# Three more random draws in a planner that writes out the instruction order, and the orders drawn again

## The chip, the cores and the metric

The kernel runs on one core of one Trainium2 chip. The metric is the device time of one execution in microseconds; the median of three runs is given. The engines are TensorE (PE, matmuls, with its weight loads PEld), VectorE (DVE), ScalarE (ACT), GpSimd (POOL) and SyncE (SP, which issues DMAs).

## The reference

`x` is 2048 rows of 512, in bf16. It is normalised, and two branches are computed from the normalised rows `xn` and multiplied:

```python
x = A_x
xn = _layernorm(x, axis=-1)
s = _A_ref(xn, A_wq, A_wk, A_wv, A_wo)   # attention
g = _silu(_B_ref(xn, B_w1, B_w2))        # silu(silu(xn @ w1) @ w2)
return x + s * g

# _A_ref: 32 heads of 16, which share one key and one value head
q = (x @ wq).reshape(B, S, 32, 16).transpose(0, 2, 1, 3)
k = x @ wk                               # [B, S, 16]
v = x @ wv
p = softmax(einsum("bhqd,bkd->bhqk", q, k) * 16 ** -0.5)
o = einsum("bhqk,bkd->bhqd", p, v)       # then heads side by side, @ wo
```

`w1` is 512 x 1792 and `w2` is 1792 x 512. The attention has 32 x 2048 x 2048 scores and as many exps, and they are nearly all of the work.

## The kernel before

**The work in tiles.** A score tile is 128 keys by 512 queries of one head. There are 32 groups (four chunks of 512 queries, four octets of heads, and two halves of an octet, even and odd heads), and 64 tiles in a group (four heads, 16 blocks of keys): 2048 score tiles. The score matmul (`s_mm`, L922 in the profile) contracts over 32 rows of the array, so up to four of them, for the four heads of a group, run side by side on the four *row* strips. Each writes a PSUM bank of its own; there are seven such banks. An eighth gathers the sums of probabilities times values of a group.

**Two ways for the exp.** A tile goes one of two ways from its bank. On the A way ScalarE takes the exp (`pa_sb`, L1819), one to three tiles in an instruction where their banks lie evenly. On the D way VectorE turns the scores into 16-bit integers, which read as bf16 are a coarse power of two (`db_sb`, L1059). When four such tiles have come together as a batch, three more copies of the batch are made with a small integer added (`ds_sb`): on GpSimd as 64-bit additions (L1268), or near the end of the last group on VectorE (L1262). The four copies, summed with four weights, give a good exp. So an A tile has one matmul with the values, a D tile four.

**The matmuls with the values** (L1348) fill 32 columns of the array each, and four, for the four heads, run side by side on the four *column* strips: a round. The products with `wq`, `w1`, `w2` and `wo` are cut in the same way (L553), a round for each 128 of the contracted dimension: four rounds for a product with `wq`, `w1` or `wo`, 14 with `w2`. The last step of such a product can also be done as four *pieces* (L660), each of which takes the place of a missing fourth tile in a visit of the row strips.

**Products.** They are called jobs: `q` (queries, with `wq`), `h` (first layer, `w1`), `z` (second layer, `w2`) and `w` (output projection, `wo`). A job holds a PSUM bank from its start until it is evicted: `q` by VectorE, `h` and `z` by a tanh on ScalarE (`t_sb`, L716) and a product on VectorE (L718). The jobs stand in a list with a `pace`, a place in the stream of score tiles ahead of which they don't begin.

**Who sets the order.** There is no order in the source. A planner, run when the kernel is built, simulates the five engines with durations and latencies of its own and places one instruction after another; each engine's list of instructions is what the chip gets, with semaphore waits for what an instruction depends on. What lies around the change:

- `Planner.best` (from L234): of an engine's ready tasks it takes the one with the lowest priority number, and the earliest in the list among equals.
- `do_S` (from L1063): places one visit of the row strips. It chooses the free banks, how many tiles go the D way, and, where only three banks are free, whether a piece of a job goes along. `PIECE_MIN` says how many steps must lie ahead for that: 4 for `z`, 9 for the other kinds, which have four steps and so never give a piece.
- `can_start` (from L1440): a job begins only where not more than `START_Z` = 4 (for `z`) or `START_H` = 11 (for other kinds) exp results wait for their matmul.
- `act_step` (from L1781): ScalarE takes a ready task of another kind (such as a tanh) ahead of the next exp, if that task is ready no later than the exp.
- `SEEDS` and `redraw` (L410): the planner's thresholds are disturbed at random. After each visit of the row strips `redraw` draws a few choices anew (`pick`), such as the number of D tiles or the bank of a job; every eight visits (`STRETCH`) the next number of `SEEDS` starts a new random sequence. So the list of seeds fixes the whole order.

Of the kernel before, what the change touches and what calls it, by code (L numbers as in the profile page):

```python
# [19 lines left out]
T_ISSUE, T_SWDGE = 450.0, 1000.0  # L20
J_BASE, J_END, MIXJ = 0.1, 1.0, 2
SEEDS = (
# [6 lines left out]
)  # L29
STRETCH, SPREAD = 8, 0.4  # L30
PIECE_MIN = {"z": 4, "h": 9, "q": 9, "w": 9}
# [33 lines left out]
PR_ZER, FIRST_T, T_ACT, K0_DV, Q0_DV = -2, 4, (1,), (), ()  # L65
PR_OTR, PR_OB = -1, -1
CHAIN, AHEAD_T, START_T = '', 0.3, 11
R_WANT, R_SPLIT, R_FIRST, R_LATE, R_TOL, R_BANK = 0.03, 0.03, 0.1, 0.1, 0.05, 0.2
NEAR, AHEAD = 18, 0.6
SWITCH, SKEW, S4 = 105.0, 10.0, 3.5  # L70
INF = float("inf")
# [13 lines left out]
START_Z, START_H = 4, 11  # L85
# [35 lines left out]
class Planner:  # L121
# [110 lines left out]
            task.on_place(task.op)  # L232

    def best(self, eng, t):  # L234
        now, soon = None, None
        for k, task in enumerate(self.tasks[eng]):
            r = self.avail(task)
            if r is None:
                continue
            if r <= t + 25.0:  # L240
                p = task.prio() if callable(task.prio) else task.prio
                key = (p if isinstance(p, tuple) else (p,), k)
                if now is None or key < now[0]:
                    now = (key, task, r)
            elif soon is None or r < soon[2]:
                soon = (0, task, r)
        return now, soon

    def finalize(self, new_sem):
# [66 lines left out]
def bass_recurrent_scan__grouped_kv_mqa__dense_activation_silu__prompt_kernel(  # L316
# [30 lines left out]
    with ExitStack() as es:  # L347
# [53 lines left out]

        pl = Planner()
        rng = [Random(SEEDS[0])] if SEEDS else []

        def vary(x):
            return x * (1.0 + SPREAD * (rng[-1].random() - 0.5)) if rng else x

        pick = dict(want=None, split=False, first=None, late=0.0, tol=0.0, early=0.0, abank=None, jbank=None)

        def redraw():  # L410
            if not rng:
                return
            r = rng[-1]
            pick.update(want=r.choice((0, 1, 2)) if r.random() < R_WANT else None, split=r.random() < R_SPLIT,
                        first=r.choice(("pv", "job")) if r.random() < R_FIRST else None,
                        late=r.random() * 200.0 if r.random() < R_LATE else 0.0,
                        tol=r.random() * 250.0 if r.random() < R_TOL else 0.0,
                        early=r.random() * 400.0 if r.random() < R_TOL else 0.0,
                        abank=r.random() if r.random() < R_BANK else None, jbank=r.random() if r.random() < R_BANK else None)
        outs = []  # L420
        PH.clear()

# [640 lines left out]
        def do_S(t):  # L1063
# [26 lines left out]
                late = []  # L1090
            if n == 3 and pl.mode != "S" and not late:
                for jb in active:
                    if jb.piece is not None and jb.pos > 0 and (jb.got or jb.end - 1 - jb.pos >= PIECE_MIN[jb.kind]):
                        pj = jb
                if pj is not None:
                    gap = min((i for i in range(4) if i not in pj.got), key=lambda i: (sum(len(left[gg, i]) for gg in range(st["gA"], min(st["gA"] + 2, NG))), i))
                    avoid.add(gap)
# [342 lines left out]
        def can_start(jb, pro):  # L1440
            near = not pro and closing()
            chain = CHAIN and not pro and jb.kind in CHAIN and any(
                not a.fixed and a.left == 0 and a.kind in "hz" and (a.ev is None or a.ev.op is None or a.ev.op.end > pl.clk[PE]) for a in active)
            if jb.pace > progress() + (AHEAD if near else AHEAD_T if chain else 1e-9):
                return False
            if any(p.op is None for p in jb.preds):
                return False
            if jb.gate is not None and not jb.gate():
                return False
            if not pro and not near and a_pressure() > (START_T if chain else START_Z if jb.kind == "z" else START_H):  # L1450
                return False
            if not jb.fixed:
                lim = 2 if pro else 1
                if len([a for a in active if not a.fixed and (a.left or not TWO)]) >= lim or not pool_free:
                    return False
                if TWO and not pro and len([a for a in active if not a.fixed]) >= 2:
                    return False
            return True
# [166 lines left out]
        def a_pressure():  # L1625
            return sum(1 for b in pa_busy if b)
# [154 lines left out]
        def act_step():  # L1781
# [10 lines left out]
            if q:  # L1792
# [15 lines left out]
                if n:  # L1808
                    q = q[:n]
                    s = min(free, key=lambda k: max(pl.ready(AC, (), [("pA", k + d)]) for d in range(n)))  # L1810
                    rx = pl.ready(AC, [("ps", u.bank) for u in q], [("pA", s + d) for d in range(n)])
            if now is not None and (rx is None or now[2] <= max(t, rx) or False):
                pl.place_task(now[1])
                return True
            if rx is not None and rx <= t + 25:
# [106 lines left out]
```

## Time and profile before

| | before |
|---|---|
| median of three runs | 665.55 us (665.44 to 666.94) |
| the profiled execution | 665.78 us, of which the span of instructions 663.9 us |
| busy PE, ACT | 652.8 us, 651.3 us |
| busy DVE, POOL | 611.2 us, 569.8 us |
| granted TensorE clock | 1.0 |

Busy time is the time in which an engine executes at least one instruction. Matmuls are pipelined, and their ends are modelled, so PE's busy time alone does not say how fast it works. The chain of waits goes back from the last instruction, at each step to what released it or to the instruction before it on its engine. In a group of instructions the name left of the arrow is what is written, the names right of it are what is read.

### The profile page before, as it was taken

Reading aid. Unit: us, or ns where it says so; the run is one execution under the profiler, and the core shown is the slowest. Engines: PE = TensorE matmul, PEld = TensorE weight load, DVE = VectorE, ACT = ScalarE, POOL = GpSimd, SP = SyncE. Lnnn points to the kernel's source line nnn. Section 1 sums busy time; section 2 is a strip of 40 time slices with the busy share of each in tenths; the row PEclk is TensorE's granted clock in tenths of the full one; section 3 lists DMA queues with packets and bytes.
Section 4 is the critical chain, followed back from the end, with each engine's and each line's share of the span. In section 5 each row is a group of like instructions: output and inputs, shape, how many; then the busy total and the mean of one; then the engine's idle time right before and its main releaser. Section 6 shows DMA issues by size and latency. Waiting matters only on the chain.

```text
span 663.9 us, 21102 instructions
## 1 busy us (share of the span) xinstructions
PE 652.8 (98%) x8927; PEld 188.5 (28%) x8928; DVE 611.2 (92%) x1081; ACT 651.3 (98%) x780; POOL 569.8 (86%) x568
## 2 busy tenths in 40 slices
PE   8899999999999999999999999999999999999997
PEld 3332222222222222222222222222222222222232
DVE  8999999999999999998999999999989999999974
ACT  7999999999999999999999999999999999999996
POOL 3059899999998898898999899899999999889983
PEclk9999999999999999999999999999999999999999
DMA  9500000000000000000000000000000000100000
GB/s 297 172 9 1 2 2 2 2 2 1 2 2 18 18 18 18 2 2 2 2 1 3 18 18 18 17 2 2 2 2 2 1 2 18 34 18 1 2 2 34
DMA packets 11500, 12.85 MB, mean 19 GB/s; under 512 B 1808, under 2 KB 10768, under 8 KB 11408
## 3 DMA queue, kind: packets, MB, share of 16 engines
q1 hardware_dynamic: 10784, 10.65, 5.0%
q8 instruction: 72, 1.18, 0.8%
q0 software_dynamic: 192, 0.46, 0.2%
q10 hardware_dynamic: 432, 0.39, 0.2%
q14 instruction: 20, 0.16, 0.1%
HBM read 8.95 MB, written 2.10 MB: 17 GB/s over the span
## 4 chain that ended last, share of the span: by engine, by line
PE 94%; DVE 3%; DMA 1%; issue 0%; ACT 0%; ACTq 0%; DVEq 0%
PE ps L1348 42%; PE ps L922 31%; PE ps L553 20%; DMA kt_sb<-kt_sb 1%; DVE db_sb L1059 1%; DMA ds_sb<-in_A_x_dram 0%; DVE stats_sb L493 0%; DVE xn_sb L528 0%; PE ps L595 0%; DVE kt_sb L609 0%; PE ps L569 0%; DVE fin_sb L772 0%; DVE xnT_sb L580 0%; DVE u_sb L718 0%; PE ps L687 0%
## 5 line engine op out<-in xcount | busy, mean ns | idle before, releaser
L1819 ACT ACTIVATE pa_sb<-ps 128x1024 bf16<-128x1024 f32 (+1 forms) x681 | 614.5, 1015 | 3.5 <-PE ps L922 2.5
L1268 POOL INT64_ADD ds_sb<-db_sb x552 | 561.8, 1040 | 52.2 <-DVE otr_sb L1408 29.1
L1059 DVE TENSOR_SCALAR db_sb<-ps 128x512 uint16<-128x512 f32 x740 | 476.0, 683 | 34.8 <-PE ps L922 19.8
L1348 PE MATMUL ps<-ds_sb,v_sb 128*32 128x512 bf16 x2220 | 259.3, 383 | 0.0
L922 PE MATMUL ps<-qt_sb,kt_sb 32*128 32x512 bf16 x2048 | 250.0, 384 | 5.1 <-DMA kt_sb<-kt_sb 1.5
L1348 PE MATMUL ps<-pa_sb,v_sb 128*32 128x512 bf16 x1312 | 230.1, 383 | 0.6 <-DVE var_sb L522 0.6
L1348 PE MATMUL ps<-db_sb,v_sb 128*32 128x512 bf16 x740 | 162.3, 384 | 0.0
L922 PEld LDWEIGHTS ps<-qt_sb,kt_sb 32*128 32x128 bf16 x2048 | 62.4, 90 | 275.9 <-ACT pa_sb L1819 147.5
L1348 PEld LDWEIGHTS ps<-ds_sb,v_sb 128*32 128x32 bf16 x2220 | 62.8, 95 | 62.0 <-issue 46.7
L553 PE MATMUL ps<-xnT_sb,w_sb 128*32 128x512 bf16 x896 | 70.8, 383 | 0.0
L1348 PEld LDWEIGHTS ps<-pa_sb,v_sb 128*32 128x32 bf16 x1312 | 56.4, 95 | 39.6 <-issue 29.2
L553 PE MATMUL ps<-w_sb,u_sb 128*32 128x512 bf16 x784 | 61.6, 383 | 0.0
L1348 PEld LDWEIGHTS ps<-db_sb,v_sb 128*32 128x32 bf16 x740 | 39.6, 94 | 24.1 <-issue 19.5
L716 ACT ACTIVATE t_sb<-ps 128x512 bf16<-128x512 f32 x72 | 44.9, 624 | 0.1
L660 PE MATMUL ps<-w_sb,u_sb 32*128 32x512 bf16 x112 | 43.1, 385 | 0.0
L718 DVE SCALAR_TENSOR_TENSOR u_sb<-t_sb,ps 128x512 bf16<-128x512 bf16 x56 | 38.4, 685 | 0.7
L1425 POOL DMA_DIRECT2D kt_sb<-kt_sb x4 | 2.3, 566 | 26.8 <-DVE kt_sb L609 16.3
L553 PEld LDWEIGHTS ps<-xnT_sb,w_sb 128*32 128x32 bf16 x896 | 18.0, 95 | 22.9 <-issue 16.3
L1404 DVE STREAM_TRANSPOSE f_sb<-ps 128x512 f32<-128x512 f32 x31 | 21.9, 707 | 2.1 <-PE ps L1348 2.0
L553 PEld LDWEIGHTS ps<-w_sb,u_sb 128*32 128x32 bf16 x784 | 14.8, 95 | 20.8 <-issue 17.0
L553 PE MATMUL ps<-wo_sb,on_sb 128*32 128x512 bf16 x256 | 19.3, 382 | 0.0
L553 PE MATMUL ps<-xnT_sb,wq_sb 128*32 128x512 bf16 x240 | 18.9, 383 | 0.0
(84 smaller groups left out, 178.2 us busy)
## 6 DMA issues: line engine op xcount, KB each, us to landing
w_sb<-in_B_w_dram SPq DMA_DIRECT2D x2, 1792.0 KB, 14.4
xr_sb<-in_A_x_dram SPq DMA_DIRECT2D x16, 128.0 KB, 2.5
out_dram<-ob_sb SPq DMA_DIRECT2D x15, 128.0 KB, 1.7
ds_sb<-in_A_x_dram SPq DMA_DIRECT2D x3, 512.0 KB, 6.7
wq_sb<-in_A_wq_dram SPq DMA_DIRECT2D x1, 512.0 KB, 4.8
wo_sb<-in_A_wo_dram SPq DMA_DIRECT2D x1, 512.0 KB, 16.8
kt_sb<-kt_sb POOLq DMA_DIRECT2D x4, 112.0 KB, 4.1
ds_sb<-in_A_x_dram SPq DMA_DIRECT2D x2, 128.0 KB, 2.8
```

What stands on the lines that cost most here:

```text
L553: last = h.matmul(bank(b)[32 * j:32 * (j + 1), 0:n], lhsT=lhs(j), rhs=rhs, start=start, stop=stop, tile_position=(0, 32 * j), skip_group_c ...
L660: return (lambda pe: pe.matmul(bank(b), lhsT=lhs(k, rows, 0, P), rhs=rhs(k, rows), start=False, stop=last, tile_position=(32 * i, 0), skip ...
L716: t1 = Task(AC, 490.0, lambda a: a.activation(t_sb[:, k, :], src, ACT.Tanh, scale=scale), [held], [("t", k)], 0, [t0])
L718: t2 = Task(DV, T_P, lambda v: v.scalar_tensor_tensor(out=dst, in0=t_sb[:, k, :], scalar=1.0, in1=src, op0=ALU.add, op1=ALU.mult), [held, ...
L922: return pe.matmul(bank(b), lhsT=kt_sb[32 * i:32 * i + 32, g % 2, kt * P:(kt + 1) * P], rhs=qt_sb[32 * i:32 * i + 32, (g // 2) % NQR, :], ...
L1059: bt.P[i] = pl.add(Task(DV, T_P, lambda v: v.tensor_scalar(db_sb[:, bt.b, i * NQ:(i + 1) * NQ], bank(b), 128.0 * LOG2E, 128.0 * (SHIFT_BET ...
L1268: whole["po"].append(pl.add(Task(PO, T_P64, lambda g, cols=cols: g.int64_add(ds_sb[:, s, cols].bitcast(U64), db_sb[:, bt.b, cols].bitcast( ...
L1348: h = pe.matmul(bank(OB)[32 * i:32 * (i + 1), cols], lhsT=lhs, rhs=rhs, start=s0, stop=s1, tile_position=(0, 32 * i), skip_group_check=True)
L1404: t1 = pl.add(Task(DV, T_TR, lambda v: v.transpose(f_sb[:, k, :], bank(OB)), [("ps", OB)], [("F", k)], 1, [norm.get(("m", g - 2))]))
L1425: kt1[c] = pl.add(Task(PO, T_SWDGE, lambda e: e.dma_start(kt_sb[DH:P, 1, cols], kt_sb[0:P - DH, 0, cols]), [("kt0", k) for k in range(4 * ...
L1819: op = pl.place(AC, 0.8333 * NQ * n + T_AF, lambda a: a.activation(pa_sb[:, s * NQ:(s + n) * NQ].rearrange("p (b n) -> p b n", n=NQ), ps3[ ...
```

## The change

The planner gets more to draw, and the list of seeds is another, with 86 numbers for 84:

- in 15% of the redraws (`R_PIECE`), the bounds for pieces are drawn: `h` and `q` may then give pieces from 1 or 2 steps ahead, `w` from 2 or 4, `z` from 2 or 3 (or, with 9, less often than before);
- in 15% (`R_START`) the bounds for beginning a job are drawn, 2, 3 or 6 for `z` and 7, 9 or 14 for the others;
- from 40 us of the planner's own time on, in 3% of the choices among several ready tasks (`R_TASK`) a random one is taken in place of the first;
- from the same time on, in 3% of the cases (`R_EXP`) in which another ready task of ScalarE would go ahead of a ready exp, the exp goes first.

As every draw comes from the same sequences and the seeds are others, nearly the whole order is new. The arithmetic, the tiles, the buffers and the transfers are the same.

```diff
 SEEDS = (
-    9089, 3239, 7631, 4203, 5265, 9254, 578, 7567, 7348, 3979, 6108, 5815, 448, 7213, 3040, 7407,
...
-    7651, 8908, 5708, 5817,
+    1291, 9250, 3587, 5855, 4291, 5471, 9169, 1197, 2615, 5657, 4085, 3409, 4598, 3191, 211, 2683,
...
+    5443, 9741, 7044, 5277, 4, 5503,
 )
-R_WANT, R_SPLIT, R_FIRST, R_LATE, R_TOL, R_BANK = 0.03, 0.03, 0.1, 0.1, 0.05, 0.2
+R_WANT, R_SPLIT, R_FIRST, R_LATE, R_TOL, R_BANK, R_PIECE, R_START = 0.03, 0.03, 0.1, 0.1, 0.05, 0.2, 0.15, 0.15
+R_TASK, R_EXP, T_FLIP = 0.03, 0.03, 40000.0
...
     def best(self, eng, t):
-        now, soon = None, None
+        now, soon, open_ = None, None, []
...
-                if now is None or key < now[0]:
-                    now = (key, task, r)
+                open_.append((key, task, r))
             elif soon is None or r < soon[2]:
                 soon = (0, task, r)
+        if open_:
+            now = min(open_, key=lambda x: x[0])
+            if len(open_) > 1 and R_TASK and self.rng and t > T_FLIP and self.rng[-1].random() < R_TASK:
+                now = open_[int(self.rng[-1].random() * len(open_))]
         return now, soon
...
+                        piece={"z": r.choice((2, 3, 9)), "h": r.choice((1, 2, 9)), "q": r.choice((1, 2, 9)), "w": r.choice((2, 4, 9))}
+                        if r.random() < R_PIECE else PIECE_MIN,
+                        start=(r.choice((2, 3, 6)), r.choice((7, 9, 14))) if r.random() < R_START else None)
...
-                    if jb.piece is not None and jb.pos > 0 and (jb.got or jb.end - 1 - jb.pos >= PIECE_MIN[jb.kind]):
+                    if jb.piece is not None and jb.pos > 0 and (jb.got or jb.end - 1 - jb.pos >= pick["piece"][jb.kind]):
...
-            if not pro and not near and a_pressure() > (START_T if chain else START_Z if jb.kind == "z" else START_H):
+            if not pro and not near and a_pressure() > (START_T if chain else (pick["start"] or (START_Z, START_H))[jb.kind != "z"]):
...
-            if now is not None and (rx is None or now[2] <= max(t, rx) or False):
+            if now is not None and (rx is None or now[2] <= max(t, rx)) and not (
+                    rx is not None and rx <= t + 25 and R_EXP and t > T_FLIP and rng[-1].random() < R_EXP):
                 pl.place_task(now[1])
```

More of the change, by code (lines that the diff above doesn't have):

```diff
@@ L403, in bass_recurrent_scan__grouped_kv_mqa__dense_activation_silu__prompt_kernel @@
         rng = [Random(SEEDS[0])] if SEEDS else []
+        pl.rng = rng
         def vary(x):
             return x * (1.0 + SPREAD * (rng[-1].random() - 0.5)) if rng else x
-        pick = dict(want=None, split=False, first=None, late=0.0, tol=0.0, early=0.0, abank=None, jbank=None)
+        pick = dict(want=None, split=False, first=None, late=0.0, tol=0.0, early=0.0, abank=None, jbank=None, piece=PIECE_MIN, start=None)
         def redraw():
@@ L418, in redraw @@
                         early=r.random() * 400.0 if r.random() < R_TOL else 0.0,
-                        abank=r.random() if r.random() < R_BANK else None, jbank=r.random() if r.random() < R_BANK else None)
+                        abank=r.random() if r.random() < R_BANK else None, jbank=r.random() if r.random() < R_BANK else None,
+                        piece={"z": r.choice((2, 3, 9)), "h": r.choice((1, 2, 9)), "q": r.choice((1, 2, 9)), "w": r.choice((2, 4, 9))}
+                        if r.random() < R_PIECE else PIECE_MIN,
+                        start=(r.choice((2, 3, 6)), r.choice((7, 9, 14))) if r.random() < R_START else None)
         outs = []
```

8 rows, old and new, of the table SEEDS are left out of this document.

## The prediction, on record before the run

> **What bounds the kernel now.** I read the page first, then the chain of waits in a short stretch, then busy time by stage, then the groups by shape, then the waits.
>
> ```profile
> span 663.9 us, 21102 instructions
> ...
> PE 652.8 (98%) x8927; PEld 188.5 (28%) x8928; DVE 611.2 (92%) x1081; ACT 651.3 (98%) x780; POOL 569.8 (86%) x568
> ...
> PE 94%; DVE 3%; DMA 1%; issue 0%; ACT 0%; ACTq 0%; DVEq 0%
> ```
>
> TensorE (PE) and ScalarE (ACT) are both busy 98% of the span. The chain of waits decides between them: 94% of it is PE, nothing is ACT. How tightly PE's work is packed is seen in a few microseconds of that chain, in order of time (start, length, what):
>
> ```profile
> 302.03 0.76 PE ps L1348 x12
> 302.79 0.33 PE ps L922 x4
> 303.12 0.76 PE ps L1348 x12
> 303.88 0.04 issue
> 303.92 0.39 PE ps L922 x3
> 304.31 0.55 PE ps L1348 x8
> 304.86 0.32 PE ps L922 x3
> ```
>
> PE alternates between two forms. L922 is a *score visit*: three or four score tiles that run side by side on row strips of the array, 0.32 us whatever their number. L1348 (and L553) is a *column visit*: rounds of four matmuls that run side by side on column strips. Eight matmuls (two rounds) take 0.55, twelve take 0.76. Two longer visits, from the chain of the whole run, give the price:
>
> ```profile
> 52.16 0.98 PE ps L1348 x16
> ...
> 68.23 1.19 PE ps L1348 x20
> ```
>
> Two rounds more than 0.55 are 0.98: 0.215 us a round, and 0.55 - 2 x 0.215 = 0.12 us for each column visit beside its rounds. These prices hold wherever PE isn't kept waiting; the piece at 303.12 shows a wait, 0.04 of "issue" and a score visit of 0.39 for 0.32, 0.11 us in all.
>
> ```profile
> 0.00:18.00 18.00, 14.10 (x203) 6.84 (x207) 15.31 (x60) 13.72 (x24) 6.37 (x13) 1.00 0.92 302
> 18.00:40.00 22.00, 19.67 (x295) 8.20 (x290) 20.18 (x56) 20.98 (x27) 2.58 (x4) 1.00 0.35 111
> 40.00:640.00 600.00, 598.99 (x8130) 166.05 (x8127) 562.91 (x940) 598.34 (x705) 550.60 (x542) 1.00 0.03 7
> 640.00:664.00 24.00, 20.06 (x312) 7.41 (x309) 12.79 (x27) 18.29 (x27) 10.23 (x11) 1.00 0.07 24
> ```
>
> Busy time by stage (columns: stretch, length, then PE, weight loads, DVE, ACT, POOL, then the granted clock, 1.00 throughout): in the middle 600 us PE is idle for 1.0 us and ACT for 1.7. So the time is PE's own work plus few waits. An order that PE works through is worth what it changes in PE's count of visits and rounds, and in the waits between them.
>
> **The change, part by part.** The arithmetic and the tiles stay; the draws decide who does what and when. The counts come from comparing the instruction orders of the two built kernels; PE's first 17 visits of any kind are the same, up to a score visit of two tiles where three stood (behind the 17.49 quoted below).
>
> *PE's static work.* Score visits rise from 638 to 645 (two tiles: 2 to 9; three instructions: 388 to 362; four: 248 to 274), +7 x 0.32 = +2.24 us. Column visits rise from 636 to 640, +4 x 0.12 = +0.48. Rounds fall from 1637.5 to 1624.5, -13 x 0.215 = -2.80. Sum: -0.1 us. The 13 rounds have two sources. Forty product matmuls, 24 with w1, 8 with wq and 8 with w2, now ride as a fourth row strip on score visits: ten rounds less. That is the first draw at work, the smaller bound for such pieces. And four tiles of exp go from the VectorE path to ACT; such a tile is summed in four pieces there (itself and three shifted copies) and in one on ACT, so 12 matmuls less, three rounds. One of 16 visits of full-array matmuls goes, with the same 148 matmuls in them: 0.1. PE is left at -0.2 us.
>
> *The other engines.* The groups by shape (busy us, mean ns, then idle before):
>
> ```profile
> L1819 ACT ACTIVATE pa_sb<-ps 128x1024 bf16<-128x1024 f32 x593 | 562.5, 1051 | 2.1 <-PE ps L922 1.2
> ...
> L1819 ACT ACTIVATE pa_sb<-ps 128x512 bf16<-128x512 f32 x73 | 41.3, 630 | 0.9 <-PE ps L922 0.8
> L1819 ACT ACTIVATE pa_sb<-ps 128x1536 bf16<-128x1536 f32 x15 | 21.9, 1483 | 0.5 <-PE ps L922 0.5
> L1767 ACT ACTIVATE pa_sb<-ps 128x256 bf16<-128x256 f32 x4 | 1.5, 412 | 0.0
> ```
>
> ```profile
> L1059 DVE TENSOR_SCALAR db_sb<-ps 128x512 uint16<-128x512 f32 x740 | 476.0, 683 | 34.8 <-PE ps L922 19.8 <-PE ps L660 9.5 <-POOL ds_sb L1268 1.0
> ...
> L1262 DVE TENSOR_SCALAR ds_sb<-db_sb 128x2048 uint16<-128x2048 uint16 x3 | 1.9, 667 | 0.0
> ```
>
> ```profile
> L1268 POOL INT64_ADD ds_sb<-db_sb x552 | 561.8, 1040 | 52.2 <-DVE otr_sb L1408 29.1 <-DVE ob_sb L784 11.3 <-PE ps L1348 6.4
> ```
>
> ACT gets 607 exps of two tiles for 593, 53 of one for 73, 14 of three for 15, and 2 quarter-size ones fewer. By busy time over count that is 14 x 0.949 - 20 x 0.566 - 1.46 - 0.75 = -0.3 us. An upper bound leaves the saved instructions out and charges four tiles at 1051 - 630 = 421 ns: +1.7. The nearest rows are the same shapes, so I take -0.3; either way ACT follows PE, whose chain doesn't run through it. The Trainium skill, "ScalarE: Activation LUTs" (section "What ACT_TABLE_LOAD costs"), gives 0.833 ns an element and 186 ns an instruction, of which back-to-back ones overlap by 93; by it four tiles more in nine instructions fewer are an estimated +0.9 us of ACT time, between the two ends.
>
> DVE loses four evictions, 4 x 476.0/740 = -2.6 us, and gets four more shifted copies at the end, 7 for 3, 4 x 1.9/3 = +2.5: nothing. POOL loses 7 shifts, 7 x 1.02 = -7.1 us, and has 52.2 us of idle time before them already: nothing. SP's queue, POOL's four copies of kt_sb and all stores keep their order.
>
> *The waits.* Here lies the unknown.
>
> ```profile
> PEld ps L922 <- ACT pa_sb L1819: 147.5, 349, 0.7
> ...
> ACT pa_sb L1819 <- PE ps L922: 2.5, 5, 0.8
> ```
>
> The 147.5 us belong to weight loads, which stand ready while the matmuls before them still run (the middle stage above has 1.0 us of idle PE for all of them); and ACT waits for scores for 2.5 us in all. What PE really loses follows from its sum. Its steady work runs from the first score to the last output round:
>
> ```profile
> 10.14 0.39 PE L922 MATMUL ps<-qt_sb,kt_sb 32*128 32x512 bf16 x3
> ...
> 17.49 0.39 PE L922 MATMUL ps<-qt_sb,kt_sb 32*128 32x512 bf16 x3 [1.50 <-DMA kt_sb<-kt_sb]
> ...
> 29.09 0.36 PE L625 MATMUL ps<-wv_sb,xnT_sb 128*128 128x16 bf16 x8
> 29.38 0.62 PE L1348 MATMUL ps<-pa_sb,v_sb 128*32 128x512 bf16 x8
> ...
> 659.24 0.38 PE L1603 MATMUL ps<-xr_sb,ident 128*128 128x512 bf16 x1 [0.16 <-issue]
> ```
>
> From 10.14 to 659.24 are 649.1 us. The visits cost 638 x 0.32 + 636 x 0.12 + 1637.5 x 0.215 = 632.5, less about 2 for the first key and query products, which lie ahead of 10.14; some 14 groups of eight small full-array matmuls at 29.38 - 29.09 = 0.29 add 4. So about 14 us are waits, an estimate. Up to 18 us the orders agree and the waits stay (1.50 of them for the copy of the keys): the first row of the stages has 3.9 us of idle PE, of which I put 3 behind 10.14. The row of 18 to 40 us shows 2.3 idle. The rest, about 9, is no idle time of a stage but spread over the middle and the end, mostly as losses of 0.1 like the one at 303.88.
>
> Of these 11 us the redrawn order replaces every one by waits of its own. Bounds: all gone, -11; or new ones. For the likeliest case I keep the middle as it is, since a kind of wait that the same rules make recurs in any order they make, and halve the 2.3 of the start: in the stretch after 18 us the changed order puts the key products between smaller score visits and does 16 matmuls with w1 where 48 stood, so scores wait less behind them: -1.1.
>
> Sum on the profiled execution's own time, 665.78 (span 663.9 and 1.9 around it): 665.8 - 0.2 - 1.1 = 664.5. That execution lies 0.2 above the median of the three runs, 665.55, so against the median the forecast is **664.3**, -0.2%. About 0.3% (2 us) is what a measurement of this kernel can tell from no change.
>
> **The rivals.**
>
> *Fewer waits (faster).* If the added draws let the order avoid half of the 11 us, PE gains 5.5 less the 1.1 counted: 660 to 663, at the middle 661.5. For it: equal work in both orders leaves waits as the one thing that more freedom can improve. Against it: most are 0.1 us, near the size of the cost of a visit itself.
>
> *Products that hold a bank longer (slower).* A product with w1 or wq has four steps; eight of them now do their last step as four pieces on four score visits. Those visits come one score visit and one column visit apart, 0.32 + 0.55 to 0.98, so the product ends four times 0.87 to 1.30, or 3.5 to 5.2 us, later and its PSUM bank, one of seven, comes free so much later. A score visit that finds one bank too few waits for the next exp: 0.42 to 0.95 us by ACT's rows. Eight times that is 3.4 to 7.6 on top of the sum's 664.5: 668 to 672. It decides the sign from 0.4 us lost at each of the eight, 3.3 in all, which ends over 2 us above the time now. Against it: 28 steps with w2 are done so already, and the middle has 1.0 us idle.
>
> *ACT as the bound.* ACT idles 1.7 us in the middle. If its stream sets the pace, its upper bound counts and PE's gain doesn't: 665.8 + 1.7 = 667.5, less than 0.3% up. The Trainium skill, "TensorEngine Tiling (Array Packing)" (section "PSUM Bottleneck"), says that with the array tiled fourfold the copying out of PSUM may become the bottleneck; by that rule this is the case to expect. The trace disagrees so far: the chain gives ACT 0%.
>
> That the draws act on nothing is excluded: the row pieces with w1 and wq are new.
>
> **How the numbers follow.** The forecast 0.39, fewer waits 0.35, longer-held banks 0.21, ACT as the bound 0.05. Faster is the second: 0.35; slower is the third: 0.21; the forecast and ACT's case lie within 0.3%: 0.44. The range reaches from 660.5, inside the second case, to 669, inside the third; the forecast's own range is 663 to 667, from the bounds of the waits at the start and of ACT's stream.
>
> **What would show it.** Right: PE's busy time within 1 us of 652.8; score visits at 0.32 and column rounds at 0.215 as now; PE idle about 1 in the middle; less than 2.3 idle between 18 and 40 us. Fewer waits: column visits of three rounds at 0.76 throughout, with few "issue" pieces in the chain, and a span under 661. Longer-held banks: waits of L922 on ACT's exps next to row pieces with w1 and wq. ACT as the bound: its share of the chain no longer 0. The sum is wrong if visits of two tiles cost more than 0.32, or if the time moves by over 2 us with PE's idle time unchanged.

## The result, and the profile after

| | before | changed |
|---|---|---|
| median | 665.50 us (665.24 to 667.40, 22 executions) | 664.63 us (664.12 to 666.04, 22 executions) |
| the profiled execution | 665.78 us | 664.51 us |

The ratio is 0.9984, with a 95% interval of 0.9977 to 0.9990: 0.16% less, 0.87 us between the medians, and so within the 0.3% that the forecast took for no change. In some executions of every kernel the mean granted clock is only 0.992 to 0.998, and many of these are longer (the kernel before, beside the repetition further down: a median of 667.22 us in 12 such executions, 665.61 in the 11 others). The page of the changed kernel, its busy times and the shares of its chain of waits (in this kernel the lines lie 8 or 9 higher: L930 is the score visit, L1356 and L561 are the column visits, L1828 is the exp):

```profile
span 662.7 us, 21093 instructions
...
PE 651.9 (98%) x8914; PEld 188.2 (28%) x8915; DVE 613.1 (93%) x1081; ACT 651.2 (98%) x771; POOL 562.2 (85%) x561
...
PE 92%; DVE 4%; ACT 2%; DMA 1%; issue 0%; ACTq 0%; DVEq 0%
```

PE is 0.9 us less busy, ACT 0.1, POOL 7.6, and DVE is 1.9 us busier. ACT has appeared in the chain, with 2%. The stages, with the same columns as before:

```profile
0.00:18.00 18.00, 14.09 (x211) 6.90 (x215) 15.39 (x60) 14.01 (x24) 6.36 (x13) 1.00 0.93 303
18.00:40.00 22.00, 19.95 (x270) 7.83 (x266) 19.93 (x55) 20.97 (x24) 4.01 (x6) 1.00 0.35 111
40.00:640.00 600.00, 599.09 (x8161) 166.30 (x8165) 562.32 (x936) 599.24 (x703) 543.44 (x535) 1.00 0.02 7
640.00:664.00 24.00, 18.76 (x288) 7.14 (x281) 15.47 (x31) 16.95 (x23) 8.43 (x9) 0.99 0.08 25
```

Between 18 and 40 us PE is idle for 2.05 us, where it was 2.33. In the middle 600 us it is idle for 0.9 (1.0 before), and ACT for 0.8 (1.7 before): in the new order ACT has as little idle time there as PE. The first score visit, the first one behind the copy of the keys, and the last one, in the timeline of PE (start, length, what):

```profile
9.89 0.39 PE L930 MATMUL ps<-qt_sb,kt_sb 32*128 32x512 bf16 x3
...
17.21 0.39 PE L930 MATMUL ps<-qt_sb,kt_sb 32*128 32x512 bf16 x3 [1.22 <-DMA kt_sb<-kt_sb]
...
652.10 0.39 PE L930 MATMUL ps<-qt_sb,kt_sb 32*128 32x512 bf16 x3
```

and the last one of the kernel before:

```profile
653.17 0.39 PE L922 MATMUL ps<-qt_sb,kt_sb 32*128 32x512 bf16 x3
```

The last score visit starts 1.07 us earlier. The first already starts 0.25 us earlier (9.89 for 10.14; up to there the orders are the same, so this is a difference of two executions), and the rest lies on the way. To see where, I took every visit of PE from the first to the last score visit, from its start to the start of the next visit, and took off the price that such a visit has when nothing holds it: 0.320 to 0.325 us for a score visit, by its tiles, and 0.116 + 0.216 a round for a column visit. What is left are PE's waits.

| us | before | changed |
|---|---|---|
| priced visits, first to last score visit | 625.5 | 625.9 |
| full-array visits | 8.8 | 8.7 |
| waits up to 18 us | 1.05 | 1.29 |
| waits from 18 to 40 us | 1.64 | 1.52 |
| waits from 40 to 640 us | 5.99 | 4.81 |
| all waits | 8.7 | 7.6 |
| from the last score visit to the end | 10.70 | 10.61 |

So the priced work rose by 0.4 and the waits fell by 1.1; in the middle alone they fell by 1.2. With 0.25 from the start and 0.1 each from full-array visits and the tail, this is the 1.2 us between the two spans. In the profile of the repetition the waits of the middle are 5.0, so that they are fewer than before doesn't hang on one execution.

Which waits became fewer is in the semaphores of the same traces. In the middle 90 visits of the kernel before, and 73 of the changed one, are followed more than 15 ns late, and in all of them the late one is a score visit behind a column visit. Nine in ten of these score visits start 45 or 46 ns after the last semaphore that they wait for, so what released it is what they waited for (these sums lie a little above the row of the table, since other visits are a few ns early):

| late score visits in the middle, and their lateness | before | changed | repetition |
|---|---|---|---|
| all | 90, 6.1 us | 73, 4.9 us | 73, 5.0 us |
| released by VectorE's eviction of a score tile (`db_sb`) | 79, 5.5 us | 61, 4.2 us | 61, 4.3 us |
| released by an exp on ScalarE (`pa_sb`) | 2, 0.1 us | 1, 0.2 us | 1, 0.2 us |

One of them, from the chain of the changed kernel; the score visit is 0.15 us late behind three evictions:

```profile
300.81 1.90 DVE db_sb L1067 x3
302.71 0.05 issue
302.75 0.39 PE ps L930 x3
```

So what the changed order gains in the middle is that fewer score visits wait for VectorE to empty a bank.

### The profile page after: what moved, and what is told of

The parts are those of the page before. It is cut to its first block, busy times and chain, and to the rows that moved or that the text cites. A ratio compares the mean times of both kernels' runs of the same rounds, so it can differ in the third digit from the quotient of the medians.

```text
span 662.7 us, 21093 instructions
## 1 busy us (share of the span) xinstructions
PE 651.9 (98%) x8914; PEld 188.2 (28%) x8915; DVE 613.1 (93%) x1081; ACT 651.2 (98%) x771; POOL 562.2 (85%) x561
## 4 chain that ended last, share of the span: by engine, by line
PE 92%; DVE 4%; ACT 2%; DMA 1%; issue 0%; ACTq 0%; DVEq 0%
PE ps L1356 41%; PE ps L930 31%; PE ps L561 20%; ACT pa_sb L1828 1%; DMA kt_sb<-kt_sb 1%; DVE db_sb L1067 1%; DVE xn_sb L536 1%; DVE stats_sb L501 0%; DMA ds_sb<-in_A_x_dram 0%; PE ps L603 0%; DVE xnT_sb L588 0%; DVE kt_sb L617 0%; DVE fin_sb L780 0%; PE ps L695 0%; DVE v_sb L642 0%
## 5 line engine op out<-in xcount | busy, mean ns | idle before, releaser
L1828 ACT ACTIVATE pa_sb<-ps 128x1024 bf16<-128x1024 f32 (+2 forms) x674 | 615.4, 1029 | 2.6 <-PE ps L930 2.0
L1276 POOL INT64_ADD ds_sb<-db_sb x545 | 554.3, 1038 | 59.7 <-DVE otr_sb L1416 28.2
L1067 DVE TENSOR_SCALAR db_sb<-ps 128x512 uint16<-128x512 f32 x736 | 475.1, 682 | 36.5 <-PE ps L930 17.7
L1356 PE MATMUL ps<-ds_sb,v_sb 128*32 128x512 bf16 x2208 | 270.9, 384 | 0.0
L930 PE MATMUL ps<-qt_sb,kt_sb 32*128 32x512 bf16 x2048 | 252.7, 384 | 3.7 <-DMA kt_sb<-kt_sb 1.2
L1356 PE MATMUL ps<-pa_sb,v_sb 128*32 128x512 bf16 x1315 | 244.8, 383 | 0.6 <-DVE v_sb L642 0.6
L1356 PE MATMUL ps<-db_sb,v_sb 128*32 128x512 bf16 x736 | 165.5, 384 | 0.0
L930 PEld LDWEIGHTS ps<-qt_sb,kt_sb 32*128 32x128 bf16 x2048 | 63.1, 91 | 276.9 <-ACT pa_sb L1828 151.9
L1356 PEld LDWEIGHTS ps<-ds_sb,v_sb 128*32 128x32 bf16 x2208 | 63.9, 95 | 62.7 <-issue 48.5
L1356 PEld LDWEIGHTS ps<-pa_sb,v_sb 128*32 128x32 bf16 x1315 | 58.7, 95 | 43.1 <-issue 32.4
L561 PE MATMUL ps<-xnT_sb,w_sb 128*32 128x512 bf16 x872 | 67.9, 382 | 0.0
L561 PE MATMUL ps<-w_sb,u_sb 128*32 128x512 bf16 x776 | 61.2, 383 | 0.0
L668 PE MATMUL ps<-w_sb,u_sb 32*128 32x512 bf16 x120 | 46.1, 385 | 0.0
L1356 PEld LDWEIGHTS ps<-db_sb,v_sb 128*32 128x32 bf16 x736 | 39.8, 95 | 20.5 <-issue 16.5
L726 DVE SCALAR_TENSOR_TENSOR u_sb<-t_sb,ps 128x512 bf16<-128x512 bf16 x56 | 38.2, 681 | 0.8
L561 PEld LDWEIGHTS ps<-xnT_sb,w_sb 128*32 128x32 bf16 x872 | 17.9, 95 | 21.3 <-issue 14.3
L561 PEld LDWEIGHTS ps<-w_sb,u_sb 128*32 128x32 bf16 x776 | 15.1, 95 | 21.3 <-issue 17.7
L561 PE MATMUL ps<-wo_sb,on_sb 128*32 128x512 bf16 x256 | 19.6, 382 | 0.0
L561 PE MATMUL ps<-xnT_sb,wq_sb 128*32 128x512 bf16 x232 | 18.1, 382 | 0.0
```

Source lines behind the costliest of these rows:

```text
L561: last = h.matmul(bank(b)[32 * j:32 * (j + 1), 0:n], lhsT=lhs(j), rhs=rhs, start=start, stop=stop, tile_position=(0, 32 * j), skip_group_c ...
L668: return (lambda pe: pe.matmul(bank(b), lhsT=lhs(k, rows, 0, P), rhs=rhs(k, rows), start=False, stop=last, tile_position=(32 * i, 0), skip ...
L726: t2 = Task(DV, T_P, lambda v: v.scalar_tensor_tensor(out=dst, in0=t_sb[:, k, :], scalar=1.0, in1=src, op0=ALU.add, op1=ALU.mult), [held, ...
L930: return pe.matmul(bank(b), lhsT=kt_sb[32 * i:32 * i + 32, g % 2, kt * P:(kt + 1) * P], rhs=qt_sb[32 * i:32 * i + 32, (g // 2) % NQR, :], ...
L1067: bt.P[i] = pl.add(Task(DV, T_P, lambda v: v.tensor_scalar(db_sb[:, bt.b, i * NQ:(i + 1) * NQ], bank(b), 128.0 * LOG2E, 128.0 * (SHIFT_BET ...
L1276: whole["po"].append(pl.add(Task(PO, T_P64, lambda g, cols=cols: g.int64_add(ds_sb[:, s, cols].bitcast(U64), db_sb[:, bt.b, cols].bitcast( ...
```

## The experiments

Except the repetition and the two that exchange planner and seeds, each run keeps the changed kernel's planned order and adds instructions to it, leaves some out or makes some narrower; the planner doesn't see the edit. An added instruction stands behind a chosen one of its engine. Next to the ratio to the kernel before stands the difference to the changed kernel (664.71 us, nine executions of its repetition) between medians of executions with a mean clock of at least 0.999; these are two to eight for each run. The runs were made in four sessions, and the kernel before has a median of 665.50 to 665.70 in them, so differences of 0.2 us in this column mean nothing.

| run | edit | time, ratio to before (95% interval) | against the changed kernel |
|---|---|---|---|
| after_again | none | 664.76, 0.9983 (0.9973 to 0.9992) | |
| pe32 | PE +6.9 us | 671.17, 1.0062 (1.0047 to 1.0077) | +6.5 |
| act14 | ACT +7.3 | 670.22, 1.0047 (1.0031 to 1.0064) | +5.5 |
| dve11 | DVE +7.7 | 668.44, 1.0033 (1.0022 to 1.0044) | +3.6 |
| pool13 | POOL +7.9 | 665.81, 0.9991 (0.9982 to 1.0001) | +1.1 |
| nopiece | no pieces of `w1`, `wq` | 666.51, 1.0005 (0.9995 to 1.0014) | +1.7 |
| newplan_oldseeds | new planner, seeds before | 677.75, 1.0178 (1.0159 to 1.0198) | +13.0 |
| oldplan_newseeds | planner before, new seeds | 674.00, 1.0118 (1.0102 to 1.0135) | +9.3 |
| peminus | PE -6.9 | 663.84, 0.9962 (0.9946 to 0.9979) | -1.9 |
| actminus | ACT -7.0 | 665.46, 0.9991 (0.9979 to 1.0003) | 0.0 |
| bothminus | PE -6.9, ACT -7.0 | 661.93, 0.9928 (0.9912 to 0.9944) | -2.8 |
| allminus | these and DVE -7.6 | 662.01, 0.9954 (0.9937 to 0.9970) | -2.8 |

**The repetition** of the changed kernel, beside the three runs that undo or exchange a part of the change:

> The changed kernel once more, beside the three below on the same chip: 664.5 to 665.0 us, 0.1 to 0.2% under the kernel before.

Measured 0.9983 (0.9973 to 0.9992): the small gain stands.

### More work on one engine

**TensorE.** 32 rounds of zeros, each right behind a full round with the values:

```diff
+        full = [o for o, ok in PVS if ok]
+        for o in full[16::len(full) // 32][:32]:
+            spare(PE, o, lambda pe: col4(pe, OB, lambda j: zer_sb[:, 32 * j:32 * (j + 1)], zer_sb[:, :], False, False), [zw])
```

> The changed kernel's own order, with 32 extra column rounds on TensorE spread over the run: four matmuls of zeros each, added into the bank of a group between two rounds, so the output is unchanged. Theory (PE's visits and rounds set the time): +32 x 0.215 = +6.9 us over the changed kernel, 671.5 us. Rival (ACT's stream sets it, PE has some slack): under +2 us. Rival (the loss is taken up by waits that PE has anyway): +3 us or less.

Measured +6.5 us for 32 x 0.215 = 6.9: nearly the whole. The price of a round stands, and nearly all of the added PE work is on the path.

**ScalarE.** 14 exps of 512 columns between those of the middle, into a tile that nobody reads:

```diff
+        exps = [o for o in pl.order[AC] if o.end - o.t0 > 850.0 and o.t0 > 30000.0]
+        for o in exps[20::len(exps) // 14][:14]:
+            prev = spare(AC, o, lambda a: a.activation(dump_sb[:, :], zer_sb[:, :], ACT.Exp), [zw] + ([prev] if prev else []))
```

> The changed kernel's own order, with 14 extra exps on ScalarE, each of 512 zeros in SBUF to a spare tile, about 0.5 us from start to start, 6.7 us of ACT time in all. Theory (PE sets the time, ACT follows it and has slack): each lengthens the wait of a score visit for a free bank, but ACT catches up; at most +2 us. Rival (ACT as the bound, or PE and ACT coupled so closely that neither has slack): +5 to +7 us.

Measured +5.5 us. In the trace each added exp takes 0.52 us to the start of the next instruction, 14 x 0.52 = 7.3 us in all, a little more than was expected. The theory that ACT only follows PE fell. The chain of waits, the added group, and two stages of this run (the profiled execution took 673.69 us, with a granted clock of 0.77 in its second stage, so its chain is read as to its kind, not its length):

```profile
ACT 68%; PE 27%; DVE 3%; DMA 1%; issue 0%; ACTq 0%
...
L1898 ACT ACTIVATE dump_sb<-zer_sb 128x512 bf16<-128x512 bf16 x14 | 9.0, 640 | 0.0
...
18.00:40.00 22.00, 20.47 (x227) 7.51 (x217) 16.93 (x49) 17.98 (x20) 1.05 (x2) 0.77 0.32 104
40.00:640.00 600.00, 594.85 (x8086) 165.07 (x8087) 557.97 (x929) 599.54 (x709) 537.64 (x529) 1.00 0.03 7
```

Between 40 and 640 us PE is idle for 5.2 us (0.9 without the edit) and ACT for 0.5. A chain that gave ACT 2% gives it 68% for 1% more work: the two engines had run at nearly the same pace all along. Read as above, the score visits that ACT's exps release late go from 0.2 us in the middle to 5.3; those that wait for VectorE's evictions stay near 4.2.

**VectorE** got 11 transposes of 701 ns, **GpSimd** 13 additions of 610 ns (half the usual size):

```diff
+            prev = spare(DV, o, lambda v: v.transpose(dump_sb[:, :], zer_sb[:, :]), [zw] + ([prev] if prev else []))
...
+            prev = spare(PO, o, lambda g: g.int64_add(
+                dump_sb[:, :].bitcast(U64), w2_sb[:, 0:2, :].rearrange("p a n -> p (a n)").bitcast(U64), 1), [w2w] + ([prev] if prev else []))
```

> The changed kernel's own order, with 11 extra transposes of a 128x512 tile of zeros on VectorE, 0.63 us from start to start, 6.9 us in all. Theory: VectorE is idle for 49 us and evicts one score tile in three; a transpose holds a bank back by 0.63 us once: +1 us or less. Rival (any engine's delay is passed on, since only seven banks lie between): +4 to +7 us.

> The changed kernel's own order, with 13 extra 64-bit additions on GpSimd of half the size of a shifted copy, about 0.52 us each, 6.8 us in all. Theory: GpSimd is idle for 100 us and its copies are summed long after they are made: 0 us. Rival (delay passed on): +3 us or more.

VectorE's added work, by its group in the profile,

```profile
L1898 DVE STREAM_TRANSPOSE dump_sb<-zer_sb 128x512 bf16<-128x512 bf16 x11 | 7.7, 701 | 0.0
```

cost 3.6 us, nearly half, and not the 1 at most that its 49 us of idle time suggested, but less than the rival's 4 to 7. GpSimd's cost 1.1 of 7.9, again between theory and rival. So VectorE's gaps don't take up the half of what is added: the late score visits that its evictions of score tiles release go from 4.2 us in the middle to 6.6.

### One part of the change undone

**The pieces.** The eight steps with `w1` and `wq` that ride on score visits as four pieces go back to a column round behind the last of these visits:

```diff
+        for (jb, k), ps4 in PIECES.items():
+            if jb.kind not in "hq":
+                continue
...
+            for o, held_, _ in ps4:
+                held_[0] = None
+            o = ps4[-1][0]
+            new = spare(PE, o, jb.whole(k, ps4[-1][2]), list(o.deps))
...
```

> The changed kernel's own order, in which the eight product steps with w1 and wq that ride as four row pieces on score visits are put back: the pieces are left out, and each step is one column round right behind the score visit that carried its last piece. Theory (rounds of PE cost what they take): +8 x 0.215 = +1.7 us, by what 32 extra rounds cost per round +1.6. Rival (a product that is finished in pieces holds its bank longer, and that costs more than the round): the product still ends at the same visit here, so the hold is the same and the rival too expects +1.7; a result at or under the changed kernel would say that a piece isn't free on a score visit.

Measured +1.7 us: the eight rounds, 8 x 0.215 = 1.7, and nothing else. The edit keeps the end of these products where it was, so it doesn't test how long they hold their banks; it shows that the pieces give their rounds back in full. What the hold costs is in the trace of the changed kernel. The four pieces of one product with `w1`, in the timeline of PE:

```profile
201.03 0.38 PE L668 MATMUL ps<-xnT_sb,w_sb 32*128 32x512 bf16 x1
...
201.91 0.39 PE L668 MATMUL ps<-xnT_sb,w_sb 32*128 32x512 bf16 x1
...
202.78 0.38 PE L668 MATMUL ps<-xnT_sb,w_sb 32*128 32x512 bf16 x1
...
203.65 0.38 PE L668 MATMUL ps<-xnT_sb,w_sb 32*128 32x512 bf16 x1
```

From the first to the last piece are 2.6 us, and 2.6 to 2.8 in all eight products. In these stretches, each with the five visits behind it, PE's visits are late by 0.4 us together, where the rival *longer-held banks* of the prediction charged 3.4 to 7.6.

**Planner and seeds exchanged.** The first has the changed planner with the seeds of before, the second the planner of before with the changed seeds (the first's edit is shown, from the changed kernel):

```diff
-    1291, 9250, 3587, 5855, 4291, 5471, 9169, 1197, 2615, 5657, 4085, 3409, 4598, 3191, 211, 2683,
...
+    9089, 3239, 7631, 4203, 5265, 9254, 578, 7567, 7348, 3979, 6108, 5815, 448, 7213, 3040, 7407,
...
```

> The changed planner with the seeds of before, so an order that nobody chose. Its counts against the changed kernel's: 637 score visits for 645, 633 column visits for 640, 1649.5 rounds for 1624.5, by the prices -8 x 0.32 - 7 x 0.12 + 25 x 0.215 = +2.0 us. Theory of the prediction (waits of the same kind recur in any order that these rules make): 666.6 us. Rival (the choice of the seeds is what keeps the waits small; the added draws do little): far more than the sum of the visits, 669 us or over.

> The planner of before with the seeds of the changed kernel, the mirror of the run above. Its counts against the changed kernel's: 638 score visits for 645, 635 column visits for 640, 1649.5 rounds for 1624.5, by the prices -7 x 0.32 - 5 x 0.12 + 25 x 0.215 = +2.5 us. Theory of the prediction (waits recur alike): 667.1 us. Rival (the choice of the seeds): 669 us or over. If only one of the two mirrors is bad, the draws matter, not the choice.

Measured +13.0 and +9.3 us: neither the draws nor the seeds are good by themselves. Of the first, the chain, ACT's waits for scores (us, times, longest) and the middle stage:

```profile
PE 67%; ACT 23%; DVE 5%; POOL 2%; DMA 1%; issue 1%; POOLq 0%; ACTq 0%; DVEq 0%
...
ACT pa_sb L1828 <- PE ps L930: 5.3, 14, 0.8
...
40.00:640.00 600.00, 595.92 (x8045) 166.18 (x8045) 553.92 (x925) 593.34 (x689) 537.37 (x529) 1.00 0.03 7
```

and of the second:

```profile
ACT pa_sb L1819 <- PE ps L922: 6.4, 18, 0.9
...
40.00:640.00 600.00, 597.31 (x8102) 166.63 (x8099) 562.23 (x939) 591.75 (x697) 545.04 (x537) 1.00 0.03 7
```

In both, PE and ACT are idle by turns: 4.1 and 6.7 us of the middle in the first, 2.7 and 8.3 in the second. By the same account of visits as above, the first has 16.6 us of waits, 627.2 of priced visits and 13.6 behind the last score visit; the second 12.7, 628.6 and 11.8. Set beside the 7.6, 625.9 and 10.6 of the changed kernel, nine of the 13 us and five of the nine are waits. Seeds that belong to another planner give an order that nobody chose. In these two the waits are not small, so the rules alone don't make them small; how the two lists in use were chosen, and how other lists would do, isn't on record.

### Less work on one engine

These leave work out, and tell whether the engine that the chain names is the one to relieve.

```diff
+        full = [o for o, ok in PVS if ok and L[o.idx - 1].mode == "C" and L[o.idx - 1].idx > 0]
+        for o in full[16::len(full) // 32][:32]:
...
+            L.remove(o)
...
+            w = NQ // 2 if len(ntanh) > 6 and len(ntanh) % 2 else NQ
+            t1 = Task(AC, 490.0, lambda a: a.activation(t_sb[:, k, 0:w], src[:, 0:w], ACT.Tanh, scale=scale),
```

The lines up to `L.remove` are the run without 32 rounds, the last two the one with half of 33 tanh; the third run has both.

> The changed kernel's own order without 32 of the rounds with the values, each from the middle of a group and of a column visit (the sums lack those tiles). Visits stay 645 and 640, rounds fall from 1624.5 to 1592.5: -32 x 0.215 = -6.9 us of PE. Theory A (PE alone sets the time; the price of an added round, 0.9 of its length, holds both ways): -6 us, 658.5. Theory B (PE and ACT are coupled through seven banks and ACT has almost no slack, as 14 added exps showed): ACT then sets the pace, -1 to -3 us.

> The changed kernel's own order, with 33 of the 72 tanh taken over half their columns only (the other half of the gate keeps an older value): 33 x 0.21 = -7.0 us of ACT. Theory A (PE alone sets the time): 0 to -0.5 us. Theory B (coupled): -1 to -4 us.

> Both edits of the two runs above in one kernel: 32 rounds with the values left out and 33 tanh over half their columns. Theory A (PE alone): the same as without the rounds alone, about -6 us. Theory B (coupled): more than the two alone together, up to -6.9 us.

Measured -1.9, 0.0 and -2.8 us: theory B holds for the first and the third, while ACT's relief alone gives nothing, as theory A said. Of the run with less PE work, the chain, its one piece between 299.08 and 304.58 us in order of time, and the middle stage:

```profile
ACT 46%; PE 45%; DVE 6%; POOL 1%; DMA 1%; issue 1%; DVEq 0%
...
299.08 5.50 ACT pa_sb L1830 x6
...
40.00:640.00 600.00, 597.38 (x8069) 164.78 (x8065) 561.72 (x937) 599.71 (x705) 546.10 (x537) 1.00 0.03 7
```

In the kernel before, the chain at 302 us was score and column visits by turns; here, in a stretch of the same time, it is six exps one behind the other. PE has 2.6 us of idle time in the middle, ACT is full to 0.3 us, and of the 6.9 us that PE gave 1.9 came through. With ACT relieved too, ACT has 2.2 us of idle time again and 4% of the chain:

```profile
PE 84%; DVE 9%; ACT 4%; POOL 1%; issue 1%; DVEq 0%
...
40.00:640.00 600.00, 597.61 (x8085) 165.33 (x8085) 561.83 (x940) 597.82 (x706) 546.97 (x537) 1.00 0.03 7
```

The gain is more than the two alone, but still under half of the dose. The account of visits says where the rest is: the priced visits fell from 625.9 to 619.0 as meant, and the waits rose from 7.6 to 11.2 (12.5 with PE alone). In the middle the late score visits that VectorE's evictions of score tiles release rose from 4.2 us to 7.1 (7.4 with PE alone), those that ACT's exps release from 0.2 to 0.7 (1.2). So most of what was lost is a wait for VectorE. The last run takes other work from VectorE; 28 of the 56 products that end a first-layer tile go over half the columns:

```diff
+            nu.append(kind == "h")
+            d = NQ // 2 if kind == "h" and sum(nu) > NFT and sum(nu) % 3 else NQ
...
-                out=dst, in0=t_sb[:, k, :], scalar=1.0, in1=src, op0=ALU.add, op1=ALU.mult),
+                out=dst[:, 0:d], in0=t_sb[:, k, 0:d], scalar=1.0, in1=src[:, 0:d], op0=ALU.add, op1=ALU.mult),
```

> The changed kernel with the 32 rounds left out and 33 tanh halved as in the run before, and besides 28 of the 56 products that end a first-layer tile (VectorE) over half the columns, at 418 ns (the row of 256 columns) for 681: 28 x 0.263 = -7.4 us of VectorE, so that the output misses those parts. All three engines that read or write the seven banks are then about 7 us lighter. Theory (TensorE, ScalarE and VectorE form one loop through the banks, and each takes over where another is relieved): the time falls clearly below the run without VectorE's part (ratio 0.9928, -3 us against the changed kernel), to -5 to -7 us against the changed kernel, ratio 0.988 to 0.991. Rival (what came back of the 7 us lies in the waits of a fixed order between TensorE and ScalarE; VectorE has its own slack): as without VectorE's part, ratio 0.992 to 0.994.

```profile
L731 DVE SCALAR_TENSOR_TENSOR u_sb<-t_sb,ps 128x512 bf16<-128x512 bf16 x28 | 19.0, 678 | 0.5 <-ACT t_sb L729 0.2
L731 DVE SCALAR_TENSOR_TENSOR u_sb<-t_sb,ps 128x256 bf16<-128x256 bf16 x28 | 11.6, 413 | 0.1
```

The group went from 38.2 us to 30.6, and the time stayed where it was: 661.93 us for 661.91, both medians taken as in the last column of the table. The ratio of 0.9954 lies above both expected ranges; between medians of executions with a mean clock of at least 0.999 it is 0.9944, and 0.9946 without VectorE's part. So the rival held as to the time: relieving these products gains nothing. VectorE's evictions of score tiles, which were not shortened, still release 7.0 us of late score visits. Whether shorter evictions, or a new plan for the lighter work, would give that time back was not tried.

## Why the prediction was right, and where its steps were not

**The size.** The forecast of 664.3 stood 1.2 us below the median of the three runs before, and 0.9 us was measured (664.63). Of its two terms, -1.1 for waits is what the account of visits gives. The other, -0.2 for PE's static work, came out as +0.4 (625.5 to 625.9), less 0.1 for full-array visits. The prediction's counts with its rounded prices gave -0.1 for visits; the account, with 0.116 and 0.216 and a price by the tiles of a visit, over the part between first and last score visit, gives +0.4. Half a microsecond of 626 is what such a table can resolve, and the 0.25 of the start, a difference of two executions, made up for much of it. That is luck, and so is the place from which the other term came.

**The place of the waits: wrong.** The prediction kept the middle as it is and halved the 2.3 us of idle PE between 18 and 40 us. That idle time fell by 0.3 and the waits in the stretch by 0.1; the middle gave 1.2. PE's stalls in the stretch, from the timeline of the kernel before (the bracket holds the idle time and what ended it),

```profile
20.96 0.39 PE L922 MATMUL ps<-qt_sb,kt_sb 32*128 32x512 bf16 x3 [0.29 <-ACT pa_sb L1819]
...
22.43 0.39 PE L922 MATMUL ps<-qt_sb,kt_sb 32*128 32x512 bf16 x3 [0.24 <-ACT pa_sb L1819]
...
28.77 0.39 PE L922 MATMUL ps<-qt_sb,kt_sb 32*128 32x512 bf16 x3 [0.40 <-DVE kt_sb L609]
...
30.52 0.39 PE L922 MATMUL ps<-qt_sb,kt_sb 32*128 32x512 bf16 x3 [0.52 <-DVE v_sb L634]
...
37.33 0.40 PE L922 MATMUL ps<-qt_sb,kt_sb 32*128 32x512 bf16 x4 [0.29 <-ACT pa_sb L1819]
...
38.80 0.39 PE L922 MATMUL ps<-qt_sb,kt_sb 32*128 32x512 bf16 x3 [0.45 <-DVE db_sb L1059]
```

and of the changed one:

```profile
21.01 0.39 PE L930 MATMUL ps<-qt_sb,kt_sb 32*128 32x512 bf16 x2 [0.51 <-DVE kt_sb L617]
...
31.54 0.62 PE L577 MATMUL ps<-ident,xn_sb 128*128 128x128 bf16 x8 [0.55 <-DVE xn_sb L536]
...
34.38 0.61 PE L603 MATMUL ps<-xnT_sb,wke_sb 128*32 128x512 bf16 x8 [0.19 <-DVE xnT_sb L588]
...
36.16 0.39 PE L930 MATMUL ps<-qt_sb,kt_sb 32*128 32x512 bf16 x3 [0.25 <-DVE db_sb L1067]
...
38.59 0.39 PE L930 MATMUL ps<-qt_sb,kt_sb 32*128 32x512 bf16 x3 [0.23 <-ACT pa_sb L1828]
```

The failed step is the halving itself: it named what would make scores wait less and not what is late next. Score visits do wait less for a bank that ACT has to empty, 0.23 us for 0.82. But PE waits for VectorE as long as before, 1.50 us for 1.37: with the keys (0.51) and an eviction (0.25), now for the normalised rows (0.55) and their transpose (0.19), where it was for the values (0.52). What fell instead, in the middle that the prediction kept as it is, are score visits that wait for VectorE's evictions of score tiles, 4.2 us for 5.5. So the sum came out by a term that was right in size by luck, and not in place. The *fewer waits* rival was right in kind, with a fifth of the middle's waits in place of half.

**"A kind of wait that the same rules make recurs in any order they make": wrong as a rule.** The two exchanged kernels put the waits at 16.6 and 12.7 us under the same rules. The changed list of seeds gives an order about as good as the one before; these two, which nobody chose, cost 9 and 13 us more than the changed kernel. The range up to 669 would not have held them.

**ACT "follows PE, whose chain doesn't run through it": wrong.** ACT's busy time changed by -0.1 us, for a term of -0.3 (its own figures add up to -0.24):

```profile
L1828 ACT ACTIVATE pa_sb<-ps 128x1024 bf16<-128x1024 f32 x607 | 574.3, 1052 | 1.8 <-PE ps L930 1.2
...
L1828 ACT ACTIVATE pa_sb<-ps 128x512 bf16<-128x512 f32 x53 | 30.0, 636 | 0.0
L1828 ACT ACTIVATE pa_sb<-ps 128x1536 bf16<-128x1536 f32 x14 | 20.1, 1491 | 0.8 <-PE ps L930 0.8
```

Busy time hides part of the change, though, since it counts an exp in full where nothing follows at once. Where the next one follows at once, the changed trace has 0.904 us from start to start for two tiles, 0.477 for one tile, 1.331 for three and 0.264 for 256 columns (a single one); by these the changed counts are 14 x 0.904 - 20 x 0.477 - 1.331 - 2 x 0.264 = +1.3 us for ACT. And 7.3 us more on ACT cost 5.5. So ACT's term is not safely hidden; the upper bound of +1.7 would have shown in the time for the most part. The estimate from the Trainium skill, "ScalarE: Activation LUTs" (section "What ACT_TABLE_LOAD costs"), +0.9, lies between the -0.1 of busy time and this +1.3. The Trainium skill, "TensorEngine Tiling (Array Packing)" (section "PSUM Bottleneck"), warns that with the array tiled fourfold the copying out of PSUM may become the bottleneck; the prediction had the trace disagree, on the chain's 0%. The runs agree with it more than the chain did: nearly all late score visits of the middle wait for VectorE to empty a bank, and with 32 rounds less on PE, ACT, which empties most of the banks, holds 46% of the chain and all but 0.3 us of the middle.

**DVE at nothing, POOL at nothing.** Of DVE's two terms the four copies came as priced:

```profile
L1067 DVE TENSOR_SCALAR db_sb<-ps 128x512 uint16<-128x512 f32 x736 | 475.1, 682 | 36.5 <-PE ps L930 17.7 <-PE ps L668 13.3 <-POOL ds_sb L1276 0.8
...
L1270 DVE TENSOR_SCALAR ds_sb<-db_sb 128x2048 uint16<-128x2048 uint16 x7 | 4.4, 686 | 0.0
```

The evictions gave 0.9 us and not 2.6 (475.1 for 476.0), and DVE ended 1.9 us busier, not level. The added copies lie behind 640 us, where DVE is busy for 15.5 us in place of 12.8, and the time from the last score visit to the end is no longer (10.6 for 10.7). To put DVE at nothing was not safe all the same: a microsecond more on it cost about 0.5 where it was spread over the middle, and the waits that fell are waits for it. POOL's 7 shifts less were hidden, as the 1.1 us for 7.9 in the other direction suggests.

**The pieces.** They are worth their rounds, 1.7 us. The *longer-held banks* rival had the hold at 3.5 to 5.2 us, where it is 2.6 to 2.8, and a late score visit for each of the eight products, where all of them together show 0.4 us.

**What the prediction set as signs.** PE busy is 651.9, within 1 of 652.8; PE is idle for 0.9 in the middle; less than 2.3 between 18 and 40 us, barely. ACT's share of the chain is no longer 0, its sign for *ACT as the bound*, and the time didn't rise. That the sign came without the result shows that it was a poor one.

## What to carry to other kernels

The chain of waits says which engine came last, not by how much: here PE had 92% of it, and taking 6.9 us from PE gave 1.9. Here two engines were each busy for over 599 of 600 us; work added to either was mostly paid, and work taken from one alone mostly not gained. So read the slack from the busy time by stage, and ask of the late visits themselves what released them: that named VectorE, which has 4% of the chain. In an order drawn by a planner the waits belong to the list and not to the rules, so forecast a new list near the old one only if there is a reason to think it as good.

## What the runs showed of the hardware that was not expected

**The clock can drop to one half for a few microseconds early in the run.** Profiles of executions with a mean clock below 0.999 show where. The granted clock is 0.91 in the first 18 us of the kernel without pieces, 0.77 and 0.93 between 18 and 40 us of the kernels with more and with less ACT work, and 1.00 from 40 to 640. In narrower stretches it is 0.50: between 14 and 17 us of the first, between 19 and 29 of the second, between 18 and 21 of the third. What triggers it is open.

**An exp from SBUF held ScalarE longer than one from PSUM.** The mean durations hardly differ, 640 ns for 512 columns of zeros in bf16 from SBUF and 636 for 512 columns in f32 from PSUM (rows above). But where the next instruction follows at once, it starts 520 ns later in the first case (519 to 521 in the 14 added exps) and 477 in the second. Whether the memory or the type makes the difference was not separated.
